# DeltaNet and maxout FFN on one core: block products for the third group's output, and a new order of the recurrent work in periods 2 to 4

## The chip, the core and the metric

The kernel runs on one core of a Trainium2 chip. A core has a matrix engine (PE, whose weight loads are listed as PEld), a vector engine (DVE), a scalar engine (ACT), a general engine (POOL) and a sync engine (SP), which here only issues DMAs. The metric is the device time of one launch in microseconds (us), all work in fp32.

## The reference

A linear recurrence with the delta rule, for 4 batches, 8 heads, 768 time steps and head dimension 48, and then a maxout network on its output:

```python
k_n = k / (np.linalg.norm(k, axis=-1, keepdims=True) + 1e-06)
for t in range(S):                       # state: (B, H, D, D), from zero
    y[:, :, t] = np.einsum('bhd,bhde->bhe', q[:, :, t], state)
    v_old = np.einsum('bhde,bhd->bhe', state, kt)
    state = state + bt[:, :, :, None] * np.einsum('bhd,bhe->bhde', kt, vt - v_old)
# x: y with the heads side by side, (B*S, H*D) = (3072, 384)
h = np.maximum(np.maximum(x @ w1, x @ w2), x @ w3)      # d_ff = 768
return h @ w_out
```

## The kernel before

**Chunks and groups.** The 768 steps are cut into 12 chunks of 64. Two chunks in all four batches are a group of 512 tokens, so there are six groups. Inside a chunk the recurrence is solved as a triangular system. For a group: loads of keys and queries turned by blocks (`load_blocks`, `turn_blocks`), Gram matrices of keys with keys and queries on PE (`gram`), keys' Gram out to DRAM as `at` and back as `x_bl` with one system per partition (`blocks`), a forward substitution on DVE (`solve`), its result out as `y_d` and back as `ut`. A chunk has four tiles of batch and head group; the unit of `gram` is half a chunk. The substitution works on 32 steps; two halves of a chunk are then joined by two small products on PE (`join_z`, `join_u`). Then, chunk by chunk, the old state is applied to keys (`old_k`) and queries (`old_q`), the new values `u` are made (`new`), the state `st` is updated (`step`), and the output `y` is made (`to_y`) and brought to DRAM, back, and turned (`y_blocks`, `read_y`, `turn_y`) into `xt`, the network's input.

**Periods.** `ffn(m)` is a generator over the network's work for group m. I call the time in which it runs period m. While it runs, the recurrent work for group m+1 is done, and the systems for group m+2 are prepared and solved. In periods 1 to 4 a yield comes behind each of the 12 hidden units: a unit is the product of `xt` with 128 columns of one weight matrix, three matmuls of 512 columns (`p_h`, L1224). `w1` has been subtracted from `w2` and `w3` (`less_first`), so the hidden value is max(0, x(w2-w1), x(w3-w1)), and x w1 w_out is added to the output by a folded matrix. An even unit ends with a relu on ACT, an odd one with a maximum into `h` on DVE. Both read the unit's bank; the "ffn" banks are two. Then comes the output.

**The output.** In periods 1 and 2 it is plain: for each of four blocks of 128 tokens nine matmuls of 384 columns (`p_o`, L1262), with an addition-free copy to `o_sb` on ACT. In periods 3 to 5 `outputs(m, hs)` does the first eight of the nine terms as a product of 2 by 2 blocks with seven block products in place of eight (`p_o`, L985, 192 columns each), the ninth term by itself (`x_times`). It needs sums of blocks of h and x (`s1` to `s4`), which DVE makes, and differences of blocks of the weights (`cross_weights`, three parts, once), and DVE adds up the results. In period 3 the sums lie in `kmore` (where turned queries and keys and later keys also lie) and in tiles called "sums". In period 5 the hidden units go by block products too (`crossed_hidden`, whose weights `cross_hidden` makes in period 4).

**Order.** The order is written by hand: each engine works in program order, and a tile of a pool is free when its last reader is done. Behind each yield i of `ffn(m)` the loop at L1505 issues recurrent work by a table. The tables `LINKS`, `FOURTH_LINKS` (period 3) and `LAST_LINKS` (period 4) map i to letters with a number:

| letter | work | letter | work |
|---|---|---|---|
| k, q | `old_k`, `old_q` | V | load of values for group m+2 |
| z, j | `join_z`, `join_u` | P, p | scaling of values for group m+2, for m+1 |
| d | `turn_t1`, for `join_u` | L, N | `load_blocks` for group m+2, m+3 |
| u, s | `new`, `step` | t | `turn_blocks` for group m+2 |
| y, x | `to_y`, `y_blocks` | g | `gram` for group m+2 |
| w, X | `read_y`, `turn_y` | K | load of plain keys of group m+2 for `step` |

For k to X and d the number is the chunk of group m+1 (0 or 1). The substitution is a generator as well: one yield behind its start (`norm`, ten small operations and the first product), 31 steps of two DVE operations (L561, L565), one yield behind the two writes of `y_d`, and two behind the eight reads of `ut`. `some(solving, n)` issues n of these; how many stand behind yield i is three, or in periods 3 and 4 what `STEPS` says. `blocks(m+2)` stands at i = 6 and `solve(m+2)` begins at i = 8.

**Values.** `prep_values(c)` divides out the norms of the keys from the values of chunk c by one multiplication, on POOL up to chunk 9 and on DVE behind it.

**State.** `step` uses for chunks 0 to 3 the keys with their padding, 64 wide, and adds to the state with one operation over 128 partitions; from chunk 4 on the keys are 48 wide, and two operations over 48 partitions each follow.

## Time and profile before

| | us |
|---|---|
| three runs | 507.44, 505.99, 507.28 |
| median | 507.28 |
| profiled execution | 506.9 |
| its span on the core | 505.2 |
| period 2 in it | 242.70 to 315.50: 72.80 |
| period 3 | 315.50 to 385.70: 70.20 |
| period 4 | 385.70 to 451.00: 65.30 |

Times within the profile are us from the start of the span. The span is what the profiler saw on the core; the execution took 1.7 more. Rows of groups give line, engine, operation, output and inputs by the program's names (partitions x elements), the number of instructions, busy time, mean ns of one, and the idle time before them with what ended most of it. A matmul in fp32 shows as two instructions on PE, so 36 matmuls are x72. Rows of the chain give start, length and what ran.

### The profile page before, as it was taken

Reading aid. Unit: us, or ns where it says so; the run is one execution under the profiler, and the core shown is the slowest. Engines: PE = TensorE matmul, PEld = TensorE weight load, DVE = VectorE, ACT = ScalarE, POOL = GpSimd, SP = SyncE. Lnnn points to the kernel's source line nnn. Section 1 sums busy time; section 2 is a strip of 40 time slices with the busy share of each in tenths; the row PEclk is TensorE's granted clock in tenths of the full one; section 3 lists DMA queues with packets and bytes.
Section 4 is the critical chain, followed back from the end, with each engine's and each line's share of the span. In section 5 each row is a group of like instructions: output and inputs, shape, how many; then the busy total and the mean of one; then the engine's idle time right before and its main releaser. Section 6 shows DMA issues by size and latency. Waiting matters only on the chain.

```text
span 505.2 us, 18676 instructions
## 1 busy us (share of the span) xinstructions
PE 484.0 (96%) x8064; PEld 338.0 (67%) x8064; DVE 361.1 (71%) x835; ACT 169.4 (34%) x320; POOL 187.1 (37%) x311
## 2 busy tenths in 40 slices
PE   7678989999999999999999999999999999999996
PEld 6467767855566555565565565555797457998895
DVE  5888799787996441799652999565998874468753
ACT  5585664885422142210152200242201032212210
POOL 7434472793391935770395880501000020000000
PEclk9855899999999999999999999999999999999999
DMA  8937869864045934544584652744224230340002
GB/s 114 205 50 214 195 142 160 198 181 137 3 120 134 191 72 77 146 119 117 112 156 104 158 137 74 149 72 96 64 54 90 47 86 15 85 94 1 0 18 47
DMA packets 109121, 53.50 MB, mean 106 GB/s; under 512 B 92208, under 2 KB 102864, under 8 KB 109040
## 3 DMA queue, kind: packets, MB, share of 16 engines
q1 hardware_dynamic: 97280, 31.78, 31.0%
q0 software_dynamic: 9216, 19.85, 16.5%
q8 instruction: 63, 1.03, 0.9%
q10 hardware_dynamic: 2544, 0.69, 0.8%
q14 instruction: 18, 0.15, 0.1%
HBM read 39.17 MB, written 13.11 MB: 103 GB/s over the span
## 4 chain that ended last, share of the span: by engine, by line
PE 76%; DVE 11%; ACT 4%; DMA 3%; SPq 3%; issue 2%; POOL 0%; DVEq 0%; ACTq 0%; POOLq 0%
PE p_h L1224 28%; PE p_o L985 13%; PE p_o L1262 12%; PE p_c L1163 5%; DVE tmp L561 3%; PE p_g L415 2%; PE p_m L905 2%; PE p_u L771 2%; PE p_k L743 2%; DVE y_p L565 2%; DMA kmore<-in_k_dram 2%; PE p_y L813 2%; PE p_s L794 2%; PE p_q L743 1%; PE p_j L726 1%
## 5 line engine op out<-in xcount | busy, mean ns | idle before, releaser
L1224 PE MATMUL p_h<-xt,w_sb 128*128 128x512 f32 (+1 forms) x450 | 186.8, 558 | 0.6 <-ACT xt L839 0.6
L1224 PEld LDWEIGHTS p_h<-xt,w_sb 128*128 128x128 f32 x450 | 82.4, 193 | 69.2 <-issue 61.6
L1238 DVE TENSOR_TENSOR h<-h,p_h 128x512 f32<-128x512 f32 (+1 forms) x42 | 25.5, 607 | 46.8 <-PE p_h L1224 46.3
L565 DVE TENSOR_TENSOR y_bl<-y_bl,tmp 128x31 f32<-128x31 f32 (+20 forms) x139 | 50.4, 363 | 4.8
L561 DVE TENSOR_TENSOR tmp<-x_bl,y_bl 128x31 f32<-128x31 f32 (+20 forms) x139 | 48.8, 351 | 3.9
L1262 PE MATMUL p_o<-wo_sb,h 128*128 128x384 f32 x144 | 48.9, 490 | 0.0
L373 POOL DMA_DIRECT2D turned<-in_q_dram x72 | 39.3, 554 | 4.6 <-POOL turned L368 3.1
L1262 PEld LDWEIGHTS p_o<-wo_sb,h 128*128 128x128 f32 x144 | 26.7, 190 | 17.2
L1234 ACT ACTIVATE h<-p_h 128x512 f32<-128x512 f32 x24 | 14.3, 597 | 69.2 <-PE p_h L1224 69.2
L263 POOL TENSOR_TENSOR w_sb<-mant,up 128x384 int32<-128x384 int32 x18 | 19.0, 1054 | 39.5 <-DVE mant L259 37.8
L415 PEld LDWEIGHTS p_g<-kqt 48*64 48x64 f32 x1216 | 24.5, 142 | 9.2 <-issue 6.3
L415 PE MATMUL p_g<-kqt 48*64 48x64 f32 (+1 forms) x1216 | 27.7, 241 | 0.9 <-ACT kqt L344 0.8
L1268 ACT COPY o_sb<-p_o 128x384 f32<-128x384 f32 x12 | 5.8, 479 | 62.6 <-PE p_o L1262 56.5
L801 DVE TENSOR_TENSOR st<-st,p_s 48x768 f32<-48x768 f32 (+1 forms) x18 | 17.1, 949 | 12.7 <-PE p_s L794 12.4
L399 DVE TENSOR_TENSOR pt<-p_g,mask 128x512 f32<-128x512 f32 x20 | 13.8, 690 | 17.0 <-PE p_g L415 16.9
L598 POOL DMA_DIRECT2D ut<-y_d x4 | 2.6, 653 | 60.6 <-DMA y_d<-y_bl 60.6
L148 POOL DMA_DIRECT2D v_t<-in_v_dram x14 | 11.6, 832 | 35.3 <-PE p_u L771 35.3
L368 POOL MEMSET turned<- 128x96 f32 x18 | 3.3, 191 | 49.4 <-DVE kqt L389 49.4
L771 PEld LDWEIGHTS p_u<-v_t,ut 64*64 64x64 f32 x768 | 13.5, 141 | 8.4 <-issue 7.3
L432 ACT COPY at<-p_g 128x512 f32<-128x512 f32 x22 | 12.8, 585 | 17.4 <-DVE pt L399 15.4
L373 POOL DMA_DIRECT2D turned<-in_k_dram x32 | 17.5, 556 | 1.2 <-POOL turned L368 1.2
L1163 PE MATMUL p_c<-xt,w_sb 128*128 128x256 f32 x72 | 17.7, 379 | 0.0
(239 smaller groups left out, 907.3 us busy)
## 6 DMA issues: line engine op xcount, KB each, us to landing
w_bits<-in_moe_w_dram SPq DMA_DIRECT2D x9, 384.0 KB, 6.2
w_bits<-in_moe_w_dram POOLq DMA_DIRECT2D x9, 384.0 KB, 5.7
turned<-in_q_dram POOLq DMA_DIRECT2D x72, 48.0 KB, 2.8
out_dram<-o_sb SPq DMA_DIRECT2D x36, 96.0 KB, 2.3
y_x<-y SPq DMA_DIRECT2D x32, 96.0 KB, 3.0
qall<-y_x SPq DMA_DIRECT2D x32, 96.0 KB, 2.8
v_t<-in_v_dram POOLq DMA_DIRECT2D x14, 192.0 KB, 5.0
at_d<-at SPq DMA_DIRECT2D x72, 32.0 KB, 3.0
```

What stands on the lines that cost most here:

```text
L263: nc.gpsimd.tensor_tensor(out=dst.bitcast(I32), in0=mant_v.bitcast(I32), in1=up_v, op=ALU.add)
L373: (queue, nc.gpsimd)[i].dma_start(out=t[p0 : p0 + 32, bb, at : at + NP * 2 * D].rearrange("p (j x) -> p j x", j=NP), in_=(k, q)[i][2 * bb ...
L415: nc.tensor.matmul(p_g[rows(bb ^ (g * i)), par, c0 : c0 + C * (1 + whole)], kq[:, 0], kq if whole else kq[:, i],)
L561: nc.vector.tensor_tensor(out=t_v, in0=row.to_broadcast(t_v.shape), in1=column.to_broadcast(t_v.shape), op=ALU.mult,)
L565: nc.vector.tensor_tensor(out=rest, in0=rest, in1=t_v, op=ALU.subtract)
L771: nc.tensor.matmul(p_v[rows(bb ^ g), g, i], ut[c % NU][rows(bb), g, h], rhs[rows(bb), g, h],)
L801: nc.vector.tensor_tensor(out=s_v[r], in0=s_v[r], in1=p_s[r, :, 0 : H * D], op=ALU.add)
L985: nc.tensor.matmul(to[:, g], a[j][:, 128 * g : 128 * (g + 1)], b[j], start=(start and g == j == 0), stop=(stop and g == 1 and j == len(a) ...
L1163: nc.tensor.matmul(to, w[stays], moves, start=(n == 0), stop=(n == len(terms) - 1))
L1224: nc.tensor.matmul(p_h, w_sb[i][:, t, f * 128 : (f + 1) * 128], xt[:, t, lo : lo + w], start=(t == 0), stop=(t == KT - 1),)
L1238: nc.vector.tensor_tensor(out=h, in0=h, in1=p_h, op=ALU.max)
L1262: nc.tensor.matmul(p_o, stays, moves, start=(n == 0), stop=(n == len(terms) - 1))
```

## The change

- `outputs` is used in period 2 as well, with `s1` and `s2` in `kmore`, `s3` in the `zs` tiles and `s4` in the `t1` tiles. `cross_weights` moves from period 3 to period 2, and its last part takes a slot of the values' pool in place of one of the turned keys'.
- Since `kmore` is then in use, the loads into it and into the keys move in period 2 (`THIRD_LINKS`: N2 behind i = 19, K behind 21). `STEPS` gives period 2 nineteen issues of the substitution; the other sixteen stand in period 3 behind i = 0 to 3.
- In period 3 the grams, joins and what follows stand elsewhere (`FOURTH_LINKS`): turned blocks behind 4 and 5, the first two grams at 5, the joins of the two chunks one unit apart (z0 behind 6, z1 and j0 behind 7, j1 behind 8), the last two grams at 8 in place of 5 of `LINKS`; `blocks(5)` at 9, `solve(5)` from 10.
- In period 4 (`LAST_LINKS`) z, j, u0, s0, y0, k1 and q1 stand one unit later. `new` of the last chunk is issued inside a block product of `outputs`, between its two halves.
- `step` of chunks 7 and 9 uses the 64-wide keys and one addition.
- Scaling of values from chunk 5 on is done by ACT in 16 multiplications of 128x48 for each chunk, with the norm as a factor for each partition; four of them (`quarter`) are issued behind a yield, as long as the queue `later` holds any.
- The second read of `ut` of each pair for group 4 goes to POOL's queue. Loads of keys for group 4 go to SP's queue. p1 stands one unit earlier.
- `crossed_hidden` issues the first two products of its first two units, and then the rest unit by unit.

```diff
--- before.py
+++ after.py
@@ -293,15 +293,27 @@
             nrms[2 * m + cc] = t[:, 16:32].rearrange("p (g h) -> p g h", g=2)
 
     def scale(c, nrm):
-        (nc.vector if c > 9 else nc.gpsimd).tensor_tensor(
+        nc.gpsimd.tensor_tensor(
             out=vts[c], in0=vts[c],
             in1=nrm[:, :, :, None].to_broadcast([128, 2, H, D]), op=ALU.mult,
         )
 
+    later = deque()
+
+    def quarter(c, nrm, g, h0):
+        for h in range(h0, h0 + H // 2):
+            nc.scalar.mul(vts[c][:, g, h], vts[c][:, g, h], nrm[:, g, h : h + 1])
+
     def prep_values(c):
 
-        if c in nrms:
-            scale(c, nrms.pop(c))
+        if c not in nrms:
+            return
+        nrm = nrms.pop(c)
+        if c < 5:
+            scale(c, nrm)
+            return
+        for n in range(4):
+            later.append((c, nrm, n // 2, H // 2 * (n % 2)))
 
 
     nrm_0 = const.tile([128, 2, 2, H], FP32, name="nrm_0")
@@ -593,7 +605,7 @@
                 for bb in range(2):
                     r0 = C * bb + BL * half
                     (
-                        (nc.sync, nc.gpsimd) if m == GROUPS - 1
+                        (nc.sync, nc.gpsimd) if m >= GROUPS - 2
                         else one_queue if m or cc else both_queues
                     )[bb].dma_start(
                         out=ut[cc][
@@ -785,7 +797,9 @@
         if c == NCH - 1:
             return
         p_s = ps_two("p_s")
-        of, w = ((dims(0), dims(1)), D) if c >= 4 else ((rows(0), rows(1)), DP)
+
+        thin = c >= 4 and c not in (7, 9)
+        of, w = ((dims(0), dims(1)), D) if thin else ((rows(0), rows(1)), DP)
         for j in range(NP):
             for g in range(2):
                 for par in range(2):
@@ -797,7 +811,7 @@
                             u[rows(half), g, h],
                         )
         s_v = st.rearrange("p b g j d -> p b (g j d)")
-        for r in of if c >= 4 else (slice(0, 128),):
+        for r in of if thin else (slice(0, 128),):
             nc.vector.tensor_tensor(
                 out=s_v[r], in0=s_v[r], in1=p_s[r, :, 0 : H * D], op=ALU.add
             )
@@ -933,8 +947,8 @@
             return
         if part == 2:
             x11, x12, x21, x22 = (w_sb[0][:, t, lr] for t in range(2) for lr in (left, right))
-            free = work.tile([128, NP, 2, 2, C], FP32, name="kqt", bufs=6)
-            free = free.rearrange("p j b i t -> p (j b i t)")
+            free = work.tile([128, 2, H, D], FP32, name="v_t", bufs=3)
+            free = free.rearrange("p g h d -> p (g h d)")
             x1, x2, x3, x4 = (free[:, HALF * n : HALF * (n + 1)] for n in range(4))
             for to, a, b in ((x3, x22, x12), (x1, x12, x11), (x2, x22, x1), (x4, x21, x2)):
                 minus(out=to, in0=a, in1=b, op=ALU.subtract)
@@ -979,8 +993,10 @@
             a.append(xt[:, t, lo : lo + 256])
         p, q = (ps_ffn([128, 2, HALF], "p_o") for _ in range(2))
 
-        def times(to, a, b, start=True, stop=True):
+        def times(to, a, b, start=True, stop=True, between=""):
             for g in range(2):
+                if g:
+                    links(m + 1, between)
                 for j in range(len(a)):
                     nc.tensor.matmul(
                         to[:, g], a[j][:, 128 * g : 128 * (g + 1)], b[j],
@@ -1014,21 +1030,31 @@
             nc.vector.tensor_tensor(out=to, in0=a, in1=b, op=how)
 
         plus, minus = ALU.add, ALU.subtract
-        n, spare = PAIRS + 1, m == GROUPS - 3
+        n, spare = PAIRS + 1, m < GROUPS - 2
         if spare:
 
             s1, s2 = (
                 [t.rearrange("p a h d -> p (a h d)")[:, 256 * j : 256 * (j + 1)] for j in range(n)]
                 for t in kmore
             )
+            if m == GROUPS - 3:
...
+            else:
+
+                s3, s4 = (
+                    [
+                        t.rearrange("p g h x -> p (g h x)")[:, 256 * j : 256 * (j + 1)]
+                        for t in ts for j in range(2)
+                    ]
+                    for ts in (zs, t1)
+                )
         else:
             xs_ready = x_sums.get(m, ())
             n -= len(xs_ready) > 0
@@ -1062,7 +1088,7 @@
         op(c11, m1, q, plus)
         store(c11, 0, 0)
         yield
-        times(p, s3, w["t3"])
+        times(p, s3, w["t3"], between="u1" if m == GROUPS - 2 else "")
         if spare:
             fourth_sums()
         m7 = held("o_sb", 2)
@@ -1147,7 +1173,7 @@
         x_sums[m] = s1, s2, s3, s4
         for j in range(FT):
             hs[j] = square("h").rearrange("p h c -> p (h c)")
-        for unit in range(2 * PAIRS):
+        def products(unit):
             j, i = divmod(unit, 2)
             w = {
                 name: t[:, 128 * j : 128 * (j + 1)]
@@ -1185,13 +1211,13 @@
             p = bank(1)
             times(p, ("b21", a12), ("c1", a13))
             result(top[:, lo], m1, p, c11)
+            yield
             p = bank(2)
             times(p, ("t3", s3))
             nc.scalar.copy(m7, p)
             p = bank(3)
             times(p, ("t1", s1))
             nc.scalar.copy(m5, p)
-            yield
             p = bank(4)
             times(p, ("t2", s2))
             nc.scalar.copy(m6, p)
@@ -1209,6 +1235,13 @@
             times(p, ("c2", a23))
             result(bottom[:, hi], m5, p)
             yield
+
+
+        units = [products(unit) for unit in range(2 * PAIRS)]
+        for unit in units[0:2]:
+            next(unit)
+        for unit in units:
+            yield from unit
 
     def ffn(m):
         xt = xts[m]
@@ -1248,7 +1281,7 @@
             early = FT
         for f in range(early, FT):
             yield from hidden(f, 0, TOK)
-        if m >= GROUPS - 3:
+        if m >= GROUPS - 4:
             yield from outputs(m, hs)
             return
         for i in range(4):
@@ -1378,25 +1411,34 @@
 
 
     LINKS = {
-        0: "k0 q0 t0 L3", 1: "t1", 2: "g0 g1 t2", 3: "z0 z1 d0 d1", 4: "j0 j1 t3 V0",
-        5: "g2 g3 p1", 6: "u0 N0", 7: "V1 N1", 8: "s0 y0 N2", 9: "x0", 10: "k1 q1",
+        0: "k0 q0 t0 L3", 1: "t1", 2: "g0 g1 t2", 3: "z0 z1 d0 d1", 4: "j0 j1 t3 V0 p1",
+        5: "g2 g3", 6: "u0 N0", 7: "V1 N1", 8: "s0 y0 N2", 9: "x0", 10: "k1 q1",
         11: "u1 w0", 13: "y1 x1 s1", 14: "X0 w1", 16: "P0", 17: "X1 K0 K1 K2 K3",
     }
+    THIRD_LINKS = {
+        **LINKS, 8: "s0 y0", 14: "w1", 15: "X0", 17: "", 18: "X1", 19: "N2",
+        21: "K0 K1 K2 K3",
+    }
     FOURTH_LINKS = {
-        **LINKS, 14: "w1", 15: "X0", 16: "", 17: "", 18: "X1",
-        21: "P0 K0 K1 K2 K3",
+        0: "k0 q0", 4: "t0 L3 t1", 5: "t2 g0 g1 p1", 6: "z0 d0", 7: "z1 d1 j0 t3",
+        8: "j1 u0 g2 g3", 9: "s0 y0 V0", 10: "x0 k1 q1", 11: "u1 w0", 12: "V1",
+        13: "y1 x1 s1", 14: "w1", 15: "X0", 16: "P0", 18: "X1", 21: "K0 K1 K2 K3",
     }
     LAST_LINKS = {
-        0: "k0 q0", 6: "p1", 8: "d0 d1 z0 z1", 9: "j0 j1", 10: "u0", 11: "s0 y0",
-        12: "x0 k1 q1", 13: "u1 w0", 14: "y1 x1", 15: "w1", 16: "X0", 19: "X1",
+        0: "k0 q0", 5: "p1", 9: "d0 d1 z0 z1", 10: "j0 j1", 11: "u0", 12: "s0 y0",
+        13: "x0 k1 q1", 14: "w0 y1 x1", 16: "w1", 17: "X0", 19: "X1",
     }
 
     STEPS = {
+        GROUPS - 4: {
+            8: 1, 9: 2, 10: 3, 11: 4,
+            14: 1, 15: 2, 16: 1, 17: 1, 20: 2, 21: 2,
+        },
         GROUPS - 3: {
-            8: 1, 9: 2, 10: 3, 11: 4,
-            14: 1, 15: 1, 16: 1, 17: 1, 20: 2, 21: 2,
+            0: 3, 1: 3, 2: 4, 3: 6,
+            10: 1, 11: 3, 14: 2, 15: 1, 16: 1, 17: 2, 20: 3, 21: 3,
         },
-        GROUPS - 2: {0: 2, 1: 3, 2: 3, 3: 3, 4: 3, 5: 3},
+        GROUPS - 2: {0: 2, 1: 3, 2: 3, 3: 3, 4: 3, 5: 5},
     }
     EARLY_LINKS = {
         9: "k0 q0", 10: "t0", 11: "t1", 12: "g0", 13: "t2", 14: "g1", 15: "t3",
@@ -1500,29 +1542,33 @@
 
 
     RECURS.update(x=y_blocks, w=read_y, X=turn_y, p=prep_values)
-    UNIT.update(t=turn_blocks, K=lambda n: load_k(n, one_queue if n > 19 else (nc.gpsimd, nc.gpsimd)))
+    UNIT.update(t=turn_blocks, K=lambda n: load_k(n, one_queue if n > 15 else (nc.gpsimd, nc.gpsimd)))
     MADE.update(V=lambda c: load_v(c, nc.gpsimd))
     for m in range(1, GROUPS):
         for i, _ in enumerate(ffn(m)):
-            if i == 0 and m < GROUPS - 2:
+            if i == 0 and m < GROUPS - 3:
                 some(solving, 3)
             if m == 1 and i in (2, 5, 8):
                 both_layers(i // 3)
-            if m == GROUPS - 2 and i in (5, 6):
-                cross_hidden(i - 4)
+            if m == GROUPS - 2 and i in (7, 8):
+                cross_hidden(i - 6)
             if m + 2 < GROUPS:
-                if i == 6:
+                if i == (9 if m == GROUPS - 3 else 6):
                     blocks(m + 2)
-                if i == 8:
+                if i == (10 if m == GROUPS - 3 else 8):
                     solving = solve(m + 2)
-            late = {GROUPS - 3: FOURTH_LINKS, GROUPS - 2: LAST_LINKS}
+            late = {
+                GROUPS - 4: THIRD_LINKS, GROUPS - 3: FOURTH_LINKS, GROUPS - 2: LAST_LINKS
+            }
             links(m + 1, late.get(m, LINKS).get(i, ""))
-            if m == GROUPS - 3 and i in (6, 7, 11):
+            if m == GROUPS - 4 and i in (6, 7, 11):
                 cross_weights((6, 7, 11).index(i))
             if m in STEPS:
                 some(solving, STEPS[m].get(i, 0))
             elif i > 7:
                 some(solving, 3 if i > 8 else 1)
+            if later:
+                quarter(*later.popleft())
     by_hand.close()
 # ---- launch: one core; inputs and outputs as the reference has them ----
 _INS = ['q', 'k', 'v', 'beta', 'moe_w1', 'moe_w2', 'moe_w3', 'moe_w_out']
```

More of the change, by code (lines that the diff above doesn't have):

```diff
@@ L1023, in outputs @@
             )
-            tiles = [
-                work.tile([128, 3, 256], FP32, name="sums", tag="w_bits", bufs=5)
-                for _ in range(3)
-            ]
-            s3, s4 = (
-                [t[:, j] for j in range(PAIRS)] + [tiles[2][:, i]]
-                for i, t in enumerate(tiles[0:2])
-            )
+            if m == GROUPS - 3:
+                tiles = [
+                    work.tile([128, 3, 256], FP32, name="sums", tag="w_bits", bufs=5)
+                    for _ in range(3)
+                ]
+                s3, s4 = (
+                    [t[:, j] for j in range(PAIRS)] + [tiles[2][:, i]]
+                    for i, t in enumerate(tiles[0:2])
+                )
+            else:
+                s3, s4 = (
+                    [
+                        t.rearrange("p g h x -> p (g h x)")[:, 256 * j : 256 * (j + 1)]
+                        for t in ts for j in range(2)
+                    ]
+                    for ts in (zs, t1)
+                )
         else:
```

## Prediction

> **What bounds the kernel now.** I read the page's totals first, then the busy time by stretches, with one stretch for each period of the loop over m (period m is the time in which `ffn(m)` runs), then the chain of work that ended last, and last the timeline around the two places where the change shortens a distance.
>
> The totals, from the page:
>
> ```profile
> PE 484.0 (96%) x8064; PEld 338.0 (67%) x8064; DVE 361.1 (71%) x835; ACT 169.4 (34%) x320; POOL 187.1 (37%) x311
> ```
>
> The stretches of periods 2, 3 and 4. After the stretch come its length, then busy us and count of PE, PEld, DVE, ACT and POOL, then the granted clock and DMA:
>
> ```profile
> 242.70:315.50 72.80, 72.80 (x1234) 42.59 (x1233) 50.92 (x118) 17.10 (x29) 43.62 (x78) 1.00 0.57 129
> 315.50:385.70 70.20, 70.20 (x1289) 49.38 (x1288) 50.85 (x121) 17.62 (x30) 9.33 (x14) 1.00 0.42 86
> 385.70:451.00 65.30, 65.30 (x1033) 45.59 (x1034) 42.06 (x91) 13.35 (x22) 2.58 (x4) 1.00 0.31 66
> ```
>
> PE is busy through every microsecond of the three periods that the change touches, at a granted clock of 1.00; DVE, the next engine, is busy 70%, 72% and 64%. So time is won here only by taking work from PE, and lost wherever PE starts to wait. Closing waits cannot win anything: there are none to close.
>
> The chain gives the price of PE's blocks (start, us, what; a matmul shows as two instructions). First the output of period 2 in plain form, then that of period 3 in seven block products, then the start of period 4:
>
> ```profile
> 290.07 6.00 PE p_o L1262 x18
> ...
> 297.87 17.61 PE p_o L1262 x54
> ...
> 362.68 6.05 PE p_o L985 x36
> ...
> 370.52 15.15 PE p_o L985 x92
> 385.67 2.84 PE p_h L1224 x6
> ...
> 390.52 20.80 PE p_h L1224 x48
> ```
>
> **What is removed from PE.** `outputs` takes the place of the plain output in period 2. Plain: 6.00 + 17.61 = 23.61. Seven products of the same shape: 6.05 + 15.15 = 21.20. Gain 2.41. The groups agree: 36 matmuls of 384 columns become 64 of 192. A matmul's two instructions start 323 ns apart at 384 columns and 163 ns apart at 192, so 72 x 0.323 = 23.3 becomes 128 x 0.163 = 20.9.
>
> Here a rule speaks against narrower products. The weight load of such an instruction shows 190 ns (group L985 LDWEIGHTS), longer than the 163 ns between two starts. The Trainium skill, "TensorE: Matmul & The Clock Gate", section "Back-to-back issue gap", says that in a real stream the spacing is set by the load and the matmul together. If loads alone paced the stream, the output would take 128 x 0.190 = 24.3, and 0.7 would be lost where 2.4 is won. The starts in periods 3 to 5 stand 163 ns apart, so the loads overlap, and I take 21.20.
>
> **What is added to PE.** The state update of chunks 7 and 9 goes from 48-wide to 64-wide weights, to save one of its two DVE additions. The chain has both widths behind a hidden unit:
>
> ```profile
> 135.26 1.08 PE p_s L794 x64
> ...
> 204.28 0.86 PE p_s L794 x64
> ```
>
> The first is chunk 3 in the 64-wide form, the second chunk 4 in the 48-wide one. Cost 0.22 each, 0.43 for two. The first unit behind a seven-product output took 2.84 (385.67) against 2.57 behind a plain one (315.48), as it waits for the bank that DVE is reading: +0.27 at the start of period 3.
>
> **What is moved on PE.** In period 3 the recurrent work breaks the hidden units eight times instead of nine, and five units follow each other. Units in a row cost 2.60 (20.80 for eight), units between breaks 2.77. That gives -0.25 in period 3 and -0.10 in period 4, where one more unit stands in the row. So PE work alone: -2.41 + 0.43 + 0.27 - 0.35 = -2.06.
>
> **What the other engines take on, and what hides it.** DVE in period 2 gets the sums (16 x 0.34 = 5.4), seven combinations (7 x 0.56 = 3.9) and the crossed weights (4.5, moved from period 3). It loses one state addition (0.95) and the solve's last 13 steps (0.7 each, 9.3), which move to period 3. 50.9 becomes 54.5 of 70.6. Period 3 gets those 9.3, gives two steps (1.8) on to period 4, and loses the 4.5 and a state addition: 53. Both stay near 76%. The order of DVE's work around the output is the one that period 3 of the trace ran without a wait, so this costs nothing there; what it costs at the start of period 3 follows below. The crossed weights' new buffer is the slot of chunk 7's values, so DVE waits there for `p_u` of chunk 7; the sums come some 0.5 later, and `s3` is done 2 before its product. Nothing.
>
> Scaling the values moves from POOL (5 x 1.5) and DVE (2 x 0.95) to 112 small ACT multiplications. No row has this form. The nearest, a 128x32 activation, takes 262 ns, and a 128x256 copy 373, so I take 0.27: four make 1.1 a unit, 30 in all, while ACT is busy 25% here. A unit's bank is wanted back 2.6 after its end and the relu takes 0.6, so up to 2.0 in front of it costs nothing. The page "ScalarE: Activation LUTs" of the Trainium skill, section "What ACT_TABLE_LOAD costs", gives 186 ns plus 0.833 ns an element, and 93 ns more for a per-partition pointer: an estimate of 0.32 each, 1.3 for four, and the same sum.
>
> The loads of the keys of group 4 move from POOL to SP, 8 issues of 0.6, ahead of the solve's write. In period 4 of the trace eight such loads were issued by 394.9, 8 before the solve's write, so nothing. The loads into `kmore` (N2) move behind the output; 16 x 0.55 on POOL end by 2 into period 3. Beginning the last period with two units' first products costs nothing and covers the sums by 1.3 more; PE had no gap there.
>
> **Where a new wait stands.** Two distances become short in period 3; the times count from its start.
>
> First, the solve's 13 late steps. In period 4 of the trace the last step ended at 402.96, 17.3 in, behind 16 steps and one scaling that follow the last output's addition. The changed queue has 15 steps there and no scaling, 0.9 each less: 15.6. From the last step to the landed `ut`:
>
> ```profile
> 403.02 1.13 SPq L586 DMA_DIRECT2D y_d<-y_bl  x2
> ...
> 406.90 2.58 POOL L598 DMA_DIRECT2D ut<-y_d  x4 [60.59 <-DMA y_d<-y_bl]
> ```
>
> The second POOL issue (407.6) plus up to 3.0 to landing is 410.6, so 7.6 from the step. That makes 23.2. PE reaches `z0` at 2.84 + 2.01 + 13.1 (five units) + 2.02 (two grams) + 2.77 = 22.7. PE waits 0.5 (between 0 and 1.2). In period 4 the same distance keeps 0.3 of cover, as `z` moves one unit back; if that is gone it costs what is missing.
>
> Second, the last pair of grams moves three units back, the next solve's start only two. Its first step needs `at` stored, `x_bl` loaded and thirteen DVE operations, and behind these in DVE's queue stands the last `h` maximum of the period, which frees the bank of the second product of `outputs`. PE has 2.77 + 1.80 + 2.77 + 2.01 + 2.77 + 1.08 + 2.70 = 15.9 between the grams and that product. The way there, in the trace of period 3 (grams ended 340.47) and of period 1 (191.21):
>
> ```profile
> 346.11 0.34 SPq L492 DMA_DIRECT2D x_bl<-at_d  x1
> ...
> 352.49 0.27 ACT L270 ACTIVATE root_bl<-x_bl 128x32 f32<-128x32 f32 x1 [1.25 <-DMA x_bl<-at_d]
> ...
> 205.88 0.26 ACT L270 ACTIVATE root_bl<-x_bl 128x32 f32<-128x32 f32 x1
> ```
>
> 340.47 to 352.49 is 12.0. Then 0.3 for the root, 4.2 for the chain (353.47 to 357.64) and 0.7 for `h`: 17.2, a wait of 1.3. In period 2 the first part was 12.6 (wait 1.9). The 4.3 that `x_bl` took in period 1 would make it 10.0 (no wait). In period 3 the load ran beside value loads issued at 344.65; these are now issued some 8 earlier. I take half of 1.3, 0.6, and keep 0 to 1.9.
>
> **Sum.** -2.06 + 0.5 + 0.6 = -0.96. The profiled execution took 506.9 (span 505.2 and 1.7 around it), which gives 505.9. The median of the three runs is 507.28, their range 505.99 to 507.44; 0.3%, about what a measurement can tell from no change, is 1.5.
>
> **Rivals.** A: both waits are covered, since transfers land as fast as the best rows. Then 506.9 - 2.06 = 504.8. For it: `x_bl` in 4.3 once; against: 15.6 + 7.6 leaves nothing for `z0`. Chance 0.30.
>
> B, slower: the second product waits long. If the transfers behind the grams take what they took in period 1, root at 14.7 behind the grams, DVE frees the bank at 19.8, a wait of 3.9: 506.9 - 2.06 + 0.5 + 3.9 = 509.2. It eats the gain from 12.3 on and makes the kernel slower by 0.3% from 13.8 on. For it: 12.0, 12.6 and 14.7 are all the trace has; against: no block loads for a later group run in this period. Chance 0.20.
>
> C: the shorter products are paced by weight loads, so that period 2 does not shrink: 506.9 + 0.7 + 0.35 + 1.1 = 509.0. The 163 ns speak against it. Chance 0.03.
>
> My forecast has 0.47. Faster by over 0.3% means below 505.4: most of A and a third of the forecast's spread, 0.38. Slower by over 0.3% means above 508.4: most of B and C, 0.18. The rest, 0.44, lies within. The range, 504.4 to 508.6, reaches from A less 0.4 of scatter between runs into the middle of B. The forecast's own is 504.9 to 507.2.
>
> **What would show it.** In the chain of the changed kernel: `p_o` of period 2 at L1001 with 21.2 in all; `p_s` of chunks 7 and 9 near 0.93; a gap ahead of `p_z` in period 3 of about 0.5; a gap ahead of the second product there, released by DVE `h`, of about 0.6. POOL without scalings after period 1. It is wrong if PE shows idle time elsewhere, above all behind ACT's multiplications, or if the output of period 2 takes more than 21.5.

## The result, and the profile after

The changed kernel takes 511.78 us (median of 22 runs, 507.99 to 516.02) against 508.25 for the kernel before (22 runs, 504.86 to 510.96) on the same chip: a ratio of 1.0064, 95% interval 1.0039 to 1.0088. It is slower by 3.5. I had forecast 505.9, reckoned from one execution of the kernel before (506.9), with 508.6 as the upper end. That kernel's median is now 1.0 above the 507.28 of its first three runs, so the ratio is the fairer comparison: 0.998 was forecast.

The totals, from the page:

```profile
PE 484.7 (95%) x8120; PEld 347.0 (68%) x8120; DVE 364.4 (71%) x855; ACT 193.7 (38%) x432; POOL 176.6 (34%) x302
```

The stretches of periods 2, 3 and 4 and of the hidden units of the last one, each begun at PE's first instruction of it (columns as in the prediction):

```profile
246.99:318.62 71.63, 70.71 (x1289) 49.80 (x1287) 50.85 (x123) 25.86 (x66) 35.10 (x67) 1.00 0.55 116
318.62:391.17 72.55, 71.31 (x1290) 50.26 (x1289) 52.99 (x131) 24.23 (x61) 10.53 (x18) 1.00 0.47 98
391.17:456.62 65.45, 65.45 (x1034) 45.54 (x1033) 41.62 (x94) 16.95 (x38) 2.58 (x4) 1.00 0.28 61
456.62:486.91 30.29, 28.75 (x133) 24.88 (x133) 24.04 (x61) 8.65 (x24) 0.00 (x0) 1.00 0.11 24
```

The last stretch in the kernel before:

```profile
450.96:479.45 28.49, 28.49 (x134) 25.01 (x133) 22.85 (x60) 8.96 (x24) 0.00 (x0) 1.00 0.06 14
```

There PE was busy in every microsecond of the four stretches. Now three of the four have a second column smaller than the first: 0.92, 1.24 and 1.54 of PE standing idle. ACT grew by 24 in all (I had 30), and DVE by 3.

The spans of two single executions (512.5 and 505.2) overstate the loss. In this one period 1 began 4.4 later than in the execution of before (162.75 against 158.35), in a part of the program that the change leaves as it was; in the other twelve traces of this study it began between 157.9 and 160.8. So from here on I compare stretches that begin with period 1. Times of the stretches, each from PE's first instruction to that of the next stretch:

| | period 1 | 2 | 3 | 4 | last, hidden | sum of 2 to last |
|---|---|---|---|---|---|---|
| before | 84.21 | 72.76 | 70.35 | 65.13 | 28.49 | 236.73 |
| before, a second profile | 84.26 | 73.01 | 70.36 | 65.13 | 28.49 | 236.99 |
| changed | 84.24 | 71.63 | 72.55 | 65.45 | 30.29 | 239.92 |
| changed less before | 0.03 | -1.13 | 2.20 | 0.32 | 1.80 | 3.19 |

The tail behind the last hidden units is 0.28 shorter (25.64 against 25.91), so 2.9 of the 3.19 is left, within the interval of the medians' 3.5 (2.0 to 4.5). Period 2 got shorter, by half of what the block products bring; period 3 and the last one lost more than that.

The chain of waits has the places (start, length, what): the joins and the output of period 2, the grams of period 3, its second product, and the start of the last period.

```profile
266.30 0.92 issue
267.22 1.20 PE p_j L738 x82
...
295.42 6.05 PE p_o L1001 x36
...
303.48 15.15 PE p_o L1001 x92
318.63 2.84 PE p_h L1257 x6
...
350.97 1.18 PE p_g L427 x48
352.15 0.93 issue
353.08 0.98 PE p_g L427 x44
...
368.62 1.23 DVE x_bl L559
370.50 3.52 PE p_o L1001 x20
...
458.43 1.11 issue
460.91 0.70 PE p_c L1189 x2
```

The output of period 2 takes 6.05 + 15.15 = 21.20, and the restart 2.84, both to the hundredth as forecast. Four waits of PE stand around them. Measured between the starts of PE's instructions they are:

- 1.10 inside the joins of period 2 (0.18 in the kernel before);
- 1.14 inside the grams of period 3;
- 0.47 ahead of the second product of period 3, which the prediction had (0.6);
- 1.70 ahead of the first product of the last period that needs the block sums of `xt`.

A wait of 0.18 for `z0` was also in the prediction (0.5).

Two of the waits are called "issue": no semaphore released PE. They stand in the middle of a run of small matmuls, 28 into the first join and 16 into the second gram, where nothing changes that an instruction could wait for. The records of DMA packets name them. PE's instructions come in packets of 16,384 bytes on a queue of their own, q8. The page has 64 of them for 16,240 records of matmuls and weight loads, and that of the kernel before 63 for 16,128 (number, MB, share of 16 engines' time):

```profile
q8 instruction: 64, 1.05, 0.9%
```

Each such wait ends 1.2 to 1.6 behind the end of a packet:

| trace | PE stands | packet on q8 | its end to PE's start |
|---|---|---|---|
| before, joins of period 2 | 261.68 to 261.87 | 259.21 to 260.32 | 1.55 |
| changed, joins of period 2 | 266.11 to 267.22 | 264.57 to 265.80 | 1.42 |
| changed, grams of period 3 | 351.93 to 353.08 | 350.84 to 351.83 | 1.25 |

PE had run out of instructions; the experiments below test that. In period 3 the change put the second join, `u`, and two grams behind each other (`j1 u0 g2 g3`, 224 matmul instructions as the trace counts them, 3.8 us without the stall), where the kernel before had at most 128 between hidden units.

The Trainium skill, "Runtime: NRT & Kernel Launch", section "Instruction fetch mechanics", has instructions streamed in blocks of 16 KiB and calls the cost of crossing a block's edge mostly hidden. The packets agree with the size. That the cost is hidden does not hold for the rows of the table, the smallest of which is 0.19.

The wait at the end is seen in the timelines of the end of period 4 of the changed kernel (start, us, instruction, in brackets the idle time before it and what ended it). SP's queue:

```profile
437.52 1.31 SPq L1022 DMA_DIRECT2D out_dram<-o_sb  x2
438.89 3.37 SPq L865 DMA_DIRECT2D y_x<-y  x4
445.38 2.53 SPq L875 DMA_DIRECT2D qall<-y_x  x4
447.95 2.53 SPq L865 DMA_DIRECT2D y_x<-y  x4
```

DVE in the same stretch:

```profile
434.49 0.95 DVE L829 TENSOR_TENSOR y<-qs,p_y 128x768 f32<-128x768 f32 x1
436.94 0.55 DVE L1030 TENSOR_TENSOR o_sb<-m,p_o 128x384 f32<-128x384 f32 x1 [1.50 <-PE p_o L1001]
...
445.36 0.95 DVE L829 TENSOR_TENSOR y<-qs,p_y 128x768 f32<-128x768 f32 x1 [6.42 <-DMA y_x<-y]
```

SP's queue in the kernel before:

```profile
427.29 3.41 SPq L851 DMA_DIRECT2D y_x<-y  x4
434.15 1.32 SPq L1006 DMA_DIRECT2D out_dram<-o_sb  x2
```

The first `y` is there at 435.44, but its writes (L865) go out at 438.89: SP has the store of the first output block (L1022) ahead of them, and that waits for DVE's addition until 437.5. In the kernel before they went out at 427.29, 0.03 behind `y`. The tile `y` has one buffer, so the second `y` waits for these writes until 445.36 although its products end at 443.93; then its own writes find SP busy with reads until 447.95. Those are the 3 us by which `xt` is late; the two first products of the last period cover part of it. DVE makes the sums for the last row of products of period 4 behind this second `y`, so that row was held up too: it takes 12.69, against 12.46 in the kernel before.

### The profile page after: what moved, and what is told of

The parts are those of the page before. It is cut to its first block, busy times and chain, and to the rows that moved or that the text cites. A ratio compares the mean times of both kernels' runs of the same rounds, so it can differ in the third digit from the quotient of the medians.

```text
span 512.5 us, 18926 instructions
## 1 busy us (share of the span) xinstructions
PE 484.7 (95%) x8120; PEld 347.0 (68%) x8120; DVE 364.4 (71%) x855; ACT 193.7 (38%) x432; POOL 176.6 (34%) x302
## 3 DMA queue, kind: packets, MB, share of 16 engines
q8 instruction: 64, 1.05, 0.9%
## 4 chain that ended last, share of the span: by engine, by line
PE 77%; DVE 7%; DMA 6%; issue 3%; ACT 3%; SPq 2%; POOL 1%; DVEq 0%; ACTq 0%; POOLq 0%
PE p_h L1257 30%; PE p_o L1001 13%; PE p_o L1295 8%; PE p_c L1189 4%; PE p_g L427 4%; PE p_m L919 2%; PE p_u L783 2%; PE p_k L755 2%; PE p_t L350 2%; PE p_y L827 2%; PE p_s L808 2%; PE p_q L755 2%; PE p_j L738 2%; DMA x_bl<-at_d 1%; PE p_z L725 1%
## 5 line engine op out<-in xcount | busy, mean ns | idle before, releaser
L577 DVE TENSOR_TENSOR y_bl<-y_bl,tmp 128x31 f32<-128x31 f32 (+20 forms) x139 | 48.5, 349 | 4.8
L573 DVE TENSOR_TENSOR tmp<-x_bl,y_bl 128x31 f32<-128x31 f32 (+20 forms) x139 | 46.8, 336 | 3.7
L1295 PE MATMUL p_o<-wo_sb,h 128*128 128x384 f32 x96 | 32.6, 489 | 0.0
L427 PEld LDWEIGHTS p_g<-kqt 48*64 48x64 f32 x1216 | 25.6, 147 | 9.5 <-issue 6.6
L610 POOL DMA_DIRECT2D ut<-y_d x8 | 5.2, 654 | 65.5 <-DMA y_d<-y_bl 65.5
L305 ACT ACTIVATE v_t<-v_t,nrm 128x48 f32<-128x48 f32 x112 | 27.2, 324 | 0.1
L1295 PEld LDWEIGHTS p_o<-wo_sb,h 128*128 128x128 f32 x96 | 17.8, 190 | 11.3
L815 DVE TENSOR_TENSOR st<-st,p_s 48x768 f32<-48x768 f32 (+1 forms) x16 | 15.2, 949 | 9.4 <-PE p_s L808 9.3
L1001 PE MATMUL p_o<-w_sb,xt 128*128 128x192 f32 x96 | 19.5, 326 | 0.0
L1001 PE MATMUL p_o<-wo_sb,h 128*128 128x192 f32 x96 | 18.7, 331 | 0.3 <-DVE h L1271 0.3
```

Of the source, the lines that this page charges most:

```text
L305: nc.scalar.mul(vts[c][:, g, h], vts[c][:, g, h], nrm[:, g, h : h + 1])
L427: nc.tensor.matmul(p_g[rows(bb ^ (g * i)), par, c0 : c0 + C * (1 + whole)], kq[:, 0], kq if whole else kq[:, i],)
L573: nc.vector.tensor_tensor(out=t_v, in0=row.to_broadcast(t_v.shape), in1=column.to_broadcast(t_v.shape), op=ALU.mult,)
L577: nc.vector.tensor_tensor(out=rest, in0=rest, in1=t_v, op=ALU.subtract)
L1001: nc.tensor.matmul(to[:, g], a[j][:, 128 * g : 128 * (g + 1)], b[j], start=(start and g == j == 0), stop=(stop and g == 1 and j == len(a) ...
L1295: nc.tensor.matmul(p_o, stays, moves, start=(n == 0), stop=(n == len(terms) - 1))
```

## The experiments

The ratios are to the kernel before, measured beside each kernel; the stretches are those of the table above.

**x0_early: the first y's writes ahead of the store.** In `LAST_LINKS`:

```
- 12: "s0 y0",    13: "x0 k1 q1",
+ 12: "s0 y0 x0", 13: "k1 q1",
```

> The changed kernel with one move: y_blocks of chunk 10 (x0) is issued behind i = 12, right behind y0, in place of i = 13, so that its four writes stand ahead of the first output store in SP's queue. Theory 1 (SP's order): in the changed kernel's trace the writes of y went out at 438.89, behind a store that waited for a DVE addition until 437.5, while y was there at 435.44; so the next y waited for its buffer (445.36 against 443.93 for the end of its products), its own write waited for SP (447.95), and the second product of the last period waited 1.70 for xt. With the writes 3 us earlier that wait falls below 0.3 and the time falls by 1.4 to 1.7, to 1.003 of the kernel before. Rival (u of the last chunk, issued inside a product, or the new start of the last period makes the wait): the wait stays at 1.4 or more and the time does not move, 1.006.

Ratio 1.0008 (0.9985 to 1.0032), 508.51. SP's timeline now has the writes first (the view begins behind the first of the four, which starts at 432.28):

```profile
432.94 1.89 SPq L865 DMA_DIRECT2D y_x<-y  x3
434.93 1.98 SPq L1022 DMA_DIRECT2D out_dram<-o_sb  x2
```

In DVE's timeline the second `y` waits for its products, not for a buffer:

```profile
440.94 0.95 DVE L829 TENSOR_TENSOR y<-qs,p_y 128x768 f32<-128x768 f32 x1 [5.19 <-PE p_y L827]
```

And the busy times of the last period's hidden units show no idle time of PE:

```profile
453.36:481.85 28.49, 28.49 (x134) 25.08 (x134) 22.85 (x60) 8.95 (x24) 0.00 (x0) 1.00 0.06 14
```

The stretch fell from 30.29 to 28.49, the value of the kernel before, and the last row of products of period 4 from 12.69 to 12.46. Theory 1 stands: 1.80 of the loss of the last period went with the order in SP's queue, and in all six kernels with `x0` early the stretch is 28.49.

The order is not the whole price, though. spread, scale_pool, pad_38 and plain_third keep it, and there the wait in the last period was 1.18, 0.42, nothing and nothing. From the first write of `y` to the second `y` it took 6.5 in the changed kernel, 5.8 in spread, 5.6 in scale_pool, and 5.2 in the last two, where `y` waited for its products alone. The order takes the slack away; how fast the writes then land decides what is paid, and why that varies is open.

**spread: period 3's work apart.** In `FOURTH_LINKS` and at the loop:

```
- 8: "j1 u0 g2 g3", 9: "s0 y0 V0", 10: "x0 k1 q1", 11: "u1 w0", 12: "V1",
+ 8: "j1 u0", 9: "g2 g3 V0", 10: "s0 y0", 11: "x0 k1 q1", 12: "u1 w0 V1",
- blocks(5) at 9, solve(5) from 10;  10: 1, 11: 3, 14: 2, 15: 1, 16: 1, 17: 2, ...
+ blocks(5) at 10, solve(5) from 11; 11: 1, 14: 3, 15: 2, 16: 2, 17: 2, ...
```

> The changed kernel with the work of period 3 behind i = 8 to 12 spread out: j1 u0 | g2 g3 V0 | s0 y0 | x0 k1 q1 | u1 w0 V1, blocks(5) behind 10 and the start of solve(5) behind 11, that is behind the last h maximum in DVE's queue. Theory 2 (PE runs out of instructions where 224 small matmul instructions stand in a row; the trace shows instruction fetches of 16 KB that end 1.3 us before the stall ends): no more than 128 stand in a row now, and the stall of 1.14 inside the grams of period 3 goes. Theory 3: the wait for the last h ahead of the second product (0.64) goes, since the solve's start no longer stands ahead of it. Both: period 3 takes 70.8 in place of 72.54, the time is 1.6 lower, 1.003 of the kernel before. Rival to theory 2 (the grams wait for a bank or a turned tile): a stall of about 1 us stays within or ahead of these grams. Rival to theory 3: the sums wait behind the solve's start in its turn and the third product waits 0.5 to 1.5.

Ratio 1.0018 (0.9989 to 1.0046), 509.05. Period 3 takes 71.34. The stall in the grams is gone, as the chain shows:

```profile
349.50 2.02 PE p_g L427 x94
```

So is the wait ahead of the second product. What is left above the 70.8 that I expected is 0.26 in a join, again behind an instruction packet, and 0.28 at the start of period 4 (0.16 in the changed kernel). The last period took 29.77 with the old order in SP's queue: 1.18 of wait, less than in the changed kernel.

**plain_third: period 2's output plain again.** `if m >= GROUPS - 3` in place of `GROUPS - 4`. This kernel leaves work out: two yields fewer leave the last step of solve(4), its writes and reads, and four loads of keys unissued, and the plain output reads weights that are already crossed. Only its period 2 can be read as a price.

> The changed kernel with the plain output in period 2 again (outputs from period 3 on); all else as changed. Theory: the seven products are worth their 2.4 in period 2, so this kernel's period 2 is 2.4 longer, its period 3 starts 0.27 faster, and the time is 2.1 higher than the changed kernel's: 1.0106 of the kernel before. Rival (the sums on DVE and the crossed weights cost period 2 as much as the products save): within 0.5 of the changed kernel, 1.006.

Ratio 1.015 (1.0124 to 1.0176), 515.71. Period 2 takes 73.89 against 71.63 with the same stall of 1.1 in the joins: 2.26, which is 2.41 less 0.16 of waiting for the bank at its end. So the products' gain is there. Period 3 took 76.91: DVE, with three steps more at its start, had the turned tiles late, PE waited 2.3 for them, and the clock was at 0.50 from 337.6 to 344.4. The time of the whole is no price of anything.

**pad_38: 38 matmuls nobody reads.** Behind i = 0 of period 3, into a tile of their own.

> The changed kernel with 38 matmuls of 64x48 more at the start of period 3, whose result nothing reads; they cost 0.65 of PE. Theory 2 (instruction fetches): the boundary at which PE runs out moves by 76 matmul instructions, so the stall of 1.14 at the 17th instruction of the second gram of period 3 is no longer there; it goes, or stands at another instruction with another length. Rival (a bank, a tile, a load): it stays at the same instruction with the same 1.1. Time between 0.5 lower and 0.65 higher than the changed kernel's, 1.005 to 1.008 of the kernel before.

Ratio 1.012 (1.008 to 1.016), 513.72; my price for the added matmuls was wrong by seven times. They all use one quarter of the array and write one place, where the kernel's small products alternate, and the trace has their 76 instructions 58 ns apart in place of 17 (which of the two makes it was not tried). PE's timeline at the start of period 3:

```profile
317.83 4.59 PE L1567 MATMUL p_d<-ident 64*64 64x48 f32 x76
322.36 4.07 PE L1257 MATMUL p_h<-xt,w_sb 128*128 128x512 f32 x5
```

The busy times there, with the granted clock as the third number from the end:

```profile
318.00:322.00 4.00, 4.00 (x74) 4.00 (x71) 2.52 (x7) 0.80 (x1) 0.00 (x0) 1.00 0.62 118
322.00:326.00 4.00, 4.00 (x13) 1.98 (x12) 0.00 (x0) 0.00 (x0) 0.00 (x0) 0.57 0.40 74
```

The clock was at 0.50 from 322.3 to 325.7, and hidden matmuls that stand 429 ns apart stood 853 ns apart in it. But what the kernel was for it answers. The stall at the 17th instruction of the second gram is gone; instead PE stands 1.00 in a join (347.01) and 0.73 in the products of `y` (359.15), 1.50 and 1.26 behind the ends of packets on q8. A delay of some 6 us could by itself hide a wait for data in the grams; it would not make two new waits behind packets, which no semaphore ends. With spread, theory 2 is shown: it is the supply of instructions. Where the edges of the packets fall decides where it shows. In pad_38 and plain_third, which move the edges, `j1 u0 g2 g3` pass as one run without a stall.

**x0_spread: both edits.**

> The changed kernel with the edits of x0_early and of spread together. Each alone left one of the two losses in place: x0_early's trace still has the stall of 1.14 in the grams and the wait of 0.54 ahead of the second product of period 3, spread's the wait of 1.18 in the last period. Theory: the two are independent, so both are gone here, periods 3 and the last take 71.3 and 28.5, and the time is 0.1 to 0.5 lower than that of the kernel before: 0.998 to 1.000. Rival (what one of them frees is taken up by the other's wait): 1.001 or more.

Ratio 1.0002 (0.9977 to 1.0026), 508.08. Stretches 71.57, 71.27, 65.35, 28.49: 236.68. The two losses are independent and both gone. That the time is still only that of the kernel before is due to two things: the join's stall in period 2 measured 1.05, and period 3 is still 0.92 longer than before.

**x0_spread_thin: 48-wide state updates for chunks 7 and 9.** `thin = c >= 4`.

> x0_spread with the state updates of chunks 7 and 9 in the 48-wide form with two additions again. Theory: PE's p_s falls from 0.93 to 0.72 in each of the two places, DVE's second addition (0.95) lies beside PE's block products, so the time falls by 0.4 more: 0.997 of the kernel before. Rival (the second addition delays DVE's block sums, which is what the 64-wide form was there to avoid): a wait of 0.3 to 0.9 ahead of the third or fourth product in period 2 or 3, and no gain.

Ratio 1.0014 (0.9992 to 1.0036), 507.9. The rival has it. Period 2 fell to 71.12, but period 3 rose to 72.72: PE waited 1.09 at the start of period 4 (0.31 in x0_spread) for a bank that DVE added late, another place than the rival named, and 0.85 for instructions inside `u` of the second chunk. In period 3 the addition saved on DVE is worth more than the 0.2 on PE.

**scale_pool and before_again: what stretches the fetch in period 2.** scale_pool has the old line `(nc.vector if c > 9 else nc.gpsimd).tensor_tensor(...)` for all chunks.

> The changed kernel with the values scaled in one operation again, on POOL up to chunk 9 and on DVE for 10 and 11, in place of 16 ACT multiplications for each chunk. Theory 4: ACT's multiplications cost PE nothing themselves, but POOL, without its 1.49 of scaling, issues the loads of the turned keys earlier in period 2, and these run beside an instruction fetch of PE there; with the scaling back on POOL the stall inside p_j of period 2 (1.10, 0.83, 0.56, 1.10, 0.52 in the five traces so far, 0.18 in that of the kernel before) is 0.3 or less, and the time 0.5 to 0.9 lower than the changed kernel's, 1.005. Rival (the length of that fetch varies by itself): the stall stays between 0.4 and 1.2, and the time within 0.3 of the changed kernel's, or above it by what DVE's two scalings cost.

> The kernel before once more, for a second profile of it. Theory 4 (the loads in period 2 of the changed kernel stretch the instruction fetch): its stall inside p_j of period 2 is again about 0.2 or less. Rival (it varies by itself): 0.4 to 1.1.

Ratio of scale_pool 1.004 (1.0013 to 1.0067), 510.4. The stall at the 29th instruction of the joins of period 2, in all traces:

| values of chunk 7 scaled by | stall in the joins of period 2 |
|---|---|
| POOL: before, before_again, scale_pool, combined, combined_thin, last_try | 0.19, 0.29, 0.26, below 0.15, 0.23, below 0.15 |
| ACT: changed, x0_early, spread, plain_third, pad_38, x0_spread, x0_spread_thin, old_start | 1.11, 0.84, 0.56, 1.11, 0.52, 1.05, 0.81, 0.72 |

The groups do not overlap; the 0.29 of before_again is a little above the 0.2 expected. Period 2 of scale_pool is 70.78, 0.85 less than the changed kernel's. The times cannot show that: the ratios 1.004 and 1.0064 have intervals that overlap, and in scale_pool's trace the stall in the grams is 1.43 and period 3 0.40 longer, the last period 1.28 shorter. POOL's timeline in scale_pool:

```profile
257.20 1.49 POOL L296 TENSOR_TENSOR v_t<-v_t,nrm 128x768 f32<-128x768 f32 x1
...
259.10 4.37 POOL L385 DMA_DIRECT2D turned<-in_k_dram  x8 [0.29 <-POOL turned L380]
```

And in the changed kernel:

```profile
257.53 1.65 POOL L148 DMA_DIRECT2D v_t<-in_v_dram  x2
...
259.66 3.82 POOL L385 DMA_DIRECT2D turned<-in_k_dram  x7 [0.30 <-POOL turned L380]
```

Without the 1.49 of scaling the loads of turned keys follow the load of values at once. The fetch began 5.36 later than in the kernel before, though PE's joins were only 4.43 later, and while its packet was under way the DMA engines were busy 1.15 of their time (packets waiting in them count) against 0.67 then. That the scaling's place decides the stall is shown. That it does so through these loads is what the packets suggest, and no run changed the loads alone. It is not the start of the fetch alone: in x0_spread_thin the packet began 1.92 ahead of the joins, as in before_again (1.96), and PE still stood 0.81.

**combined and combined_thin.** `if c < 9` for POOL's scaling on top of x0_spread, and the two steps of solve(5) behind i = 17 moved behind 21; combined_thin also has `thin = c >= 4`.

> x0_spread with the values up to chunk 8 scaled by POOL again (so that POOL pauses in period 2 as in the kernel before) and with the two steps of solve(5) behind i = 17 of period 3 moved behind i = 21, so that the last additions and the last turn of that output come earlier on DVE. Theories 1, 2 and 4 together: period 2 takes 70.8 (x0_spread 71.57, scale_pool 70.78), period 3 71.0, period 4 65.35, the last one 28.49: 1.1 to 1.4 less than the kernel before from period 2 on, 0.997 to 0.998 of its time. Rival (POOL's pause does not matter once grams and joins are spread, or another fetch takes the stall over): 0.5 or more stays in a joins or grams stall, 1.000.

> combined with the 48-wide state update of chunks 7 and 9 too. In x0_spread_thin, PE waited 0.92 at the start of period 4 for an addition that DVE made late, with the steps behind i = 17 ahead of it; these now stand behind i = 21. Theory: PE saves 0.43 and the wait is below 0.3: 0.3 to 0.5 less than combined, 0.996 to 0.997 of the kernel before. Rival (the second state addition, 0.95 on DVE, is on the path at the end of period 3 or 2 whatever the order): a wait of 0.5 to 1.0 at the start of period 4 or 3, and the time is that of combined or above.

Ratios 0.9999 (0.9971 to 1.0028) and 1.0001 (0.9969 to 1.0033). Neither gained. The join's stall is 0.23 or less in both, and combined_thin's period 2 is 70.54. In combined it is 74.08, by something else. Its timelines of DVE:

```profile
285.27 3.45 DVE L559 TENSOR_TENSOR x_bl<-x_bl,bl 128x1024 f32<-128x1024 f32 x1
288.64 0.68 DVE L1271 TENSOR_TENSOR h<-h,p_h 128x512 f32<-128x512 f32 x1
```

of POOL:

```profile
286.14 1.49 POOL L296 TENSOR_TENSOR v_t<-v_t,nrm 128x768 f32<-128x768 f32 x1
```

and of PE:

```profile
286.47 1.11 PE L755 MATMUL p_q<-st,kqt 48*64 48x48 f32 x64
289.37 2.93 PE L1257 MATMUL p_h<-xt,w_sb 128*128 128x512 f32 x3 [1.79 <-DVE h L1271]
```

POOL scales chunk 8 as soon as the solve's start has its norms, which is just when DVE prepares `x_bl`. That operation takes 1.23 alone and 3.45 here, `h` is late, PE waits 1.79 and then runs 3.4 us at half clock. The profiled execution of combined was the slowest of its twelve (511.41), so its 74.08 need not be what most have. In combined_thin the same two met and POOL gave way (1.66 in place of 1.49, DVE 1.23). In the two profiles of the kernel before POOL came to it at 294.6 and 295.6, when DVE's operation was long over. The Trainium skill, "SBUF — State Buffer", section "Terms", has VectorE and GpSimd share a pair of ports that one of them holds for a whole instruction while the other is blocked. The 3.45 is more than 1.23 + 1.49, so it fits that only with some loss besides. Combined_thin lost its gain in period 3 (73.23): 1.24 ahead of the products of `y` and 1.17 at the start of period 4. Both also lose in period 4 (66.19 and 66.03, against 65.35 in x0_spread): with the two steps moved behind i = 21 DVE is later with `h`, and PE waits for it twice, some 0.2 and 0.44.

**old_start: the last period begun as before.**

> The changed kernel with the last period begun as in the kernel before: the first unit's products one after the other. Theory (the two units' first products cover the block sums of xt for 1.3): the wait ahead of the first product that needs the sums grows from 1.70 to about 3.0, and the last period's hidden units take 31.6 in place of 30.29. Rival (the new start covers nothing): they take 30.3.

This is one run. The wait is 2.62 in place of 1.70, and behind it the clock was at 0.50 from 456.7 to 460.1; together 32.90 in place of 30.29. The new start covers the 1.3 that I had: PE's work ahead of the wait is 2.59 with it and 1.30 without. The waits differ by only 0.9 since PE could go on 3.92 into the period here and 4.29 in the changed kernel. With `x0` early there is nothing to cover: 28.49 is also what the kernel before took.

**last_try.** x0_spread with `if c < 5 or c == 7` for POOL's scaling and `thin = c >= 4 and c != 9`.

> x0_spread with two edits: the values of chunk 7 alone are scaled by POOL again (the pause in period 2 that keeps its loads off PE's instruction fetch; chunk 8's stays on ACT, since on POOL it ran at 286.1 in the trace of combined, beside DVE's 1.23 of preparing x_bl, which took 3.45), and the state update of chunk 7 alone is 48 wide again (period 2 took 70.54 with it in combined_thin; in period 3 it made DVE late, so chunk 9 stays 64 wide). Expected: period 2 in 70.5, period 3 in 71.3, period 4 in 65.35, the last one's hidden units in 28.49, in all 235.6 against 236.7 and 237.0 in the two profiles of the kernel before: 1.1 to 1.4 less, 0.997 to 0.998 of its time. Rival (the loads or a fetch fall together again in another place): 0.5 or more in a new stall, 0.999 or more.

```profile
243.44:313.78 70.34, 70.34 (x1289) 49.53 (x1287) 51.82 (x124) 22.11 (x50) 36.42 (x68) 1.00 0.53 117
313.78:385.05 71.27, 71.04 (x1289) 50.13 (x1288) 53.11 (x131) 24.15 (x61) 10.50 (x18) 1.00 0.45 100
385.05:450.42 65.37, 65.36 (x1032) 45.63 (x1033) 43.29 (x96) 16.92 (x38) 2.57 (x4) 1.00 0.31 68
450.42:478.91 28.49, 28.49 (x134) 25.09 (x133) 22.76 (x60) 8.93 (x24) 0.00 (x0) 1.00 0.06 14
```

In sum 235.47, 1.26 and 1.52 less than the two profiles of the kernel before, as expected: period 2 is 2.4 to 2.7 shorter, the whole gain of the products, and period 3 is still 0.9 longer and period 4 0.24. The ratio is 0.9985 (0.9956 to 1.0014), 506.71 against 507.68. The interval holds 1, so the runs alone do not show that it beats the kernel before; the changed kernel's interval (1.0039 to 1.0088) lies clear of it.

## Why the prediction was wrong

**The work of PE was sized right, in its largest terms.** The products: 21.20 as forecast; period 2 of last_try, with the 48-wide update of chunk 7 and no stall, is 2.42 and 2.67 below the two profiles of before, against 2.41. The 64-wide update: 0.93 against 0.72 in the chain, 0.21. The restart: 2.84. ACT's multiplications: four took 1.01 (I had 1.1 for them), and no wait of PE follows one of them; back to back they start 0.23 apart. One term for DVE was off without harm: thirteen steps left period 2 with some 12, not 9.3, so DVE has 50.9 there and not 54.5.

The prediction's estimate from the Trainium skill, "ScalarE: Activation LUTs", section "What ACT_TABLE_LOAD costs", was 0.32 for one multiplication; the group's mean is 324 ns.

**The sum of breaks was wrong in period 4.** I put -0.10 there for one more unit in the row; it measured +0.32. The longer row of units saved 0.20. But `s0 y0` now breaks a row of block products, one break more than before, which costs 0.20 (21.70 for the products in x0_early, 21.50 in the kernel before); the last row was held up by 0.23, which belongs to the order in SP's queue; and `p_q` at the start took 0.11 more. I priced breaks between hidden units and none between products.

**The two waits that I foresaw were there and small.** 0.18 for `z0` (0.5 forecast) and 0.47 ahead of the second product (0.6): `x_bl`'s root came 11.2 behind the grams, less than the 12.0 that I took. The rival that made the kernel slower by this path (14.7) did not come.

**Three steps failed.** First, "costs nothing and covers the sums by 1.3 more; PE had no gap there", of the last period. In period 4 `x0` moves one unit later together with `k1` and `q1`, from behind i = 12 to behind 13; the list of the change leaves it out, and the prediction has no term for it. With that move the writes of `y` pass behind the store in SP's queue, which waits for DVE: 1.80 in the changed kernel, and 0 with the one line undone (x0_early). Second, PE's breaks were priced as if instructions were always at hand. That a run of small instructions can outrun the fetch was not in any term: 1.14 in period 3, gone with the run of 224 broken up (spread), elsewhere with instructions put ahead (pad_38). The kernel before had it too, and I passed over it: its list of waits has `PE p_u L771 <- issue: 1.2, 2, 1.0`, ahead of period 1, where PE goes on at 65.65, 1.27 behind the end of a packet. Third, moving the scaling off POOL was costed on ACT, where it is free, and not on what POOL does sooner: 0.92 in period 2 (1.10 against 0.18), down to 0.26 with the scaling back (scale_pool). How the scaling's place brings it about stays open.

With the 0.42 of period 4 (0.32 in place of -0.10), 1.80 + 1.14 + 0.92 + 0.42 is 4.28, and the two foreseen waits gave back 0.45: 505.9 + 3.83 is 509.7. The profiled execution with the first period of before comes to 506.9 + 0.03 + 3.19 less 0.28 for a shorter tail, 509.8.

## What to carry to other kernels

Here one engine is busy all the time. The saving on it came as reckoned, and the price lay in what the other queues then did at other times: follow each moved instruction through every queue it passes, DMA issues above all, and follow also what an engine does earlier when work is taken from it. Small matmuls use up instructions fast: keep runs of them short, and read "issue" rows of a chain beside the packets of the instruction queue. A hidden unit between runs of 128 was not enough in every case (0.5 to 1.1 in the joins of period 2). Where a wait of PE reached 1.8 us, add the clock that it cost behind it, 1.6 or more here.

## What the runs showed that I had not expected

PE's instruction packets: in the stalls inside a run of small matmuls that are named above, PE went on 1.2 to 1.9 us behind the end of a packet of 16,384 bytes, in kernels as different as before and pad_38.

The granted clock: in plain_third, pad_38, combined and old_start it went to 0.50 in the middle of a dense kernel, in windows of 3.4 us or twice that, behind waits of 1.8 to 2.6 us or behind a run of 4.6 us of small matmuls; each window of 3.4 cost 1.6 to 1.8, the double one 2.5. Waits of 1.1 to 1.7 (the changed kernel) did not bring it about.

DVE and POOL at once: the same operation of 128x1024 took 3.45 beside POOL's scaling in combined and 1.23 beside it in combined_thin, where POOL took 1.66 in place of 1.49. What decides between the two is open.
